# Seventy further matmuls on TensorE behind the last FFN tile

## The chip, the cores and the metric

The kernel runs on one core of one Trainium2 chip. The metric is the device time of one execution in microseconds (us). The core has four compute engines that concern us: TensorE (in the profile PE for the matmuls and PEld for the weight loads), VectorE (DVE), ScalarE (ACT) and GpSimd (POOL). DMA transfers are issued by SyncE's queue (SP, in the profile SPq). A matmul has a stationary operand, loaded as weights, and a moving operand, whose columns stream past the weights; its result goes to PSUM, a memory of 8 banks, of which one bank holds 128 x 512 float32.

## The reference

The kernel computes a transformer layer whose two branches run in parallel, for 2048 tokens of 576 channels:

```python
x = A_x
xn = _layernorm(x, axis=-1)
return x + _A_ref(xn, A_wqkv, A_wo) + _B_ref(xn, B_w1, B_b1, B_w2, B_b2)
```

`_A_ref` is attention of 32 heads of 18 channels over a dilated local window (8 positions, 2 apart) and an output projection `wo`. `_B_ref` is a feed-forward network (FFN): `relu(xn @ w1 + b1)` squared, times `w2`, plus `b2`, with 4608 hidden channels.

## The kernel before

The tokens are worked on in 4 blocks of 512 (`NB`, `TB`). The hidden channels of the FFN are cut into 36 tiles of 128 (`NF`), so there are `NT` = 144 FFN tiles in all, numbered through the blocks. The loop at the end of `block_kernel` calls `step(n)` for each of them and once more for the tail. A step asks for the weights of tile n + 2 (`load_w`: 128x640 of `w1` into `raw1`, 128x576 of `w2` into `raw2`, three buffers each), splits the `w1` tile of n + 1, runs `ffn1(n)`, splits the `w2` tile of n, runs a piece of attention or of the output projection, and runs `ffn2(n - 2)`: `LAG` = 2 steps lie between the first and the second matrix product of a tile.

Float32 precision is made from float32r, a float32 format that TensorE takes at full rate. Each operand is split into a high part and a rest: ScalarE copies float32 to float32r (line 118, or line 124 for `w2` and `wo`), VectorE subtracts (line 120 or 126). A product is then three products: high by high, high by rest, rest by high. All matmuls of the steady part have 128 stationary columns, and most have 512 moving columns:

- line 492 (`ffn1`): 14 matmuls into one bank of the pool `pw`, whose three buffers are all named `wk`; ScalarE reads the bank (lines 494 to 498: relu, and the square twice, into `hh` and `r`) and VectorE makes the rest `hl` (line 499).
- line 515 (`accumulate`): 14 matmuls a tile into five banks `y`, which stay open for a whole block; the output projection adds to the same banks, with the weights `wos` (a single buffer, written by line 124).
- line 372 (`three`): the projections to q, k and v, 56 matmuls for each quarter of the heads in each block, with the moving width from the list `WIDE` in line 39: 448, 512, 384 and 384 columns in the first block, 512, 512, 384 and 320 in the others.
- line 172: transposes of 128x128 in the opening. Line 621: bfloat16 matmuls on a zeroed tile in the opening, 128x512, repeated with nothing read from them.

In the last part of the last block the steps also hold the five chunks of the output projection (`o_weights`, `o_chunk`, `o_acc`, lines 665 to 668): the chunk is prepared into a buffer named `kv` two steps before it is multiplied.

Most instructions are ordered by a scheduler from their dependencies. Within `manual_schedule` the engines named there keep the order of the program; the opening is written so, and the tail (`ffn2_tail`), which closes the last two tiles. In the tail each bank `y` is completed in turn and stored, and for the last group of output channels the tail takes two fresh buffers `wk` and computes two halves of 256 columns, six matmuls each (line 564). VectorE adds each half to the residual (line 566), and the queue stores it (line 567). All engines take the instructions of their own list strictly in order.

The last buffer taken from `pw` ahead of the tail is that of the last `ffn1`; then come the two of line 561.

Of the kernel before, what the change touches and what calls it, by code (L numbers as in the profile page):

```python
# [8 lines left out]
F32 = mybir.dt.float32  # L9
F32R = mybir.dt.float32r  # L10
BF16 = mybir.dt.bfloat16
AF = mybir.ActivationFunctionType
ALU = mybir.AluOpType
ET = mybir.EngineType
AX = mybir.AxisListType

P = 128
S, D, F = 2048, 576, 4608
H, DH, W, DIL = 32, 18, 8, 2
TB = 512  # L20
NB = S // TB
NJ = TB // P
NC = 5
# [20 lines left out]
def block_kernel(ctx: ExitStack, tc: tile.TileContext, x, xt, wqkv, wo, w1, b1, w2, b2, out):  # L44
# [624 lines left out]
    def step(n):  # L669
        if 2 < n + 2 < NT:  # L670
            load_w(n + 2)
        if 0 < n < NT - 1:
            split_w1(n + 1)
        for f, a in pre.get(n, []):
            f(*a)
        if 0 < n < NT:
            ffn1(n)
        if n < NT:
            split_w2(n)
        busy = n >= NF and n % NF in (LAG - 1, LAG - 2)  # L680
        for f, a in mid.get(n, []):
            f(*a)
        if not busy:
            piece()
            piece()
        if n == NT:
            with tc.manual_schedule(engines={ET.PE, ET.DVE}):
                ffn2_tail([NT - 2, NT - 1])
        elif n >= LAG:
            ffn2(n - LAG)  # L690
        if not busy:
            piece()

    for n in range(NT + 1):
        with opening() if n < 7 else ExitStack():
            step(n)


_OUTS = [((1, S, D), 'float32')]

# [42 lines left out]
```

## Time and profile before

| what | value |
|---|---|
| median of 3 runs | 1161.35 us (1161.29 to 1161.71) |
| the profiled execution: time | 1161.42 us |
| the profiled execution: span, first to last instruction | 1159.7 us |
| TensorE matmul busy, share of the span | 1154.3 us, 100% |
| weight loads busy | 966.5 us, 83% |
| VectorE, ScalarE, GpSimd busy | 847.5, 602.2, 18.3 us |
| matmuls | 5227 |
| granted TensorE clock, mean | 1.000 |

A profile row for a group of instructions names the line, the engine, the operation, the tiles written and read, the shapes and the count; behind the bar come the busy time in us, the mean of one in ns, and the idle time of the engine before them with what ended it. A row of the timeline begins with the start and the length in us, counted from the start of the span. Matmul records overlap, since a matmul's results are still draining while the next one's columns enter: the length of a record is not the time that a matmul adds to a stream. The chain of waits is followed back from the last instruction, at each step to what released it. A row of windows begins with the stretch, its length, then the busy time and count of the matmuls and of the loads, the granted clock, the DMA share and GB/s.

### The profile page before, as it was taken

The numbers are of one execution on the slowest core, as the hardware profiler recorded it, in microseconds if no ns is written. First come the engines' busy times: TensorE is split into PE (matmuls) and PEld (weight loads), VectorE is DVE, ScalarE is ACT, GpSimd is POOL, SyncE is SP. The second block draws the span as 40 slices with busy tenths as digits, with TensorE's granted clock in tenths as the row PEclk, the third lists the DMA queues.
The fourth block names the chain that finished last, engine by engine and source line by source line (L and its number), as shares of the span: only waits on it lengthen the run. The fifth ranks groups of instructions, "written<-read, shape, count | busy, mean of one in ns | idle before, by whom it ended". The sixth has DMA issues, their size and how long they took to land.

```text
span 1159.7 us, 14795 instructions
## 1 busy us (share of the span) xinstructions
PE 1154.3 (100%) x5227; PEld 966.5 (83%) x5227; DVE 847.5 (73%) x1373; ACT 602.2 (52%) x1086; POOL 18.3 (2%) x32
## 2 busy tenths in 40 slices
PE   9999999999999999999999999999999999999998
PEld 7888888888888888888888888888888888888887
DVE  6967798892788686995287969698528795957453
ACT  7645545563545454555364546555535455545552
POOL 2000000000000100000000010000000000000000
PEclk9999999999999999999999999999999999999999
DMA  8656547432656655444266665644326645353421
GB/s 290 214 170 223 177 133 234 123 112 63 209 190 206 212 183 198 132 115 120 63 234 203 203 216 153 214 111 125 106 75 232 221 131 184 108 181 111 121 63 51
DMA packets 89674, 185.90 MB, mean 160 GB/s; under 512 B 9984, under 2 KB 33280, under 8 KB 88320
## 3 DMA queue, kind: packets, MB, share of 16 engines
q1 hardware_dynamic: 89312, 184.58, 50.1%
q8 instruction: 41, 0.67, 0.2%
q10 hardware_dynamic: 288, 0.38, 0.1%
q14 instruction: 33, 0.27, 0.1%
HBM read 165.96 MB, written 18.96 MB: 159 GB/s over the span
## 4 chain that ended last, share of the span: by engine, by line
PE 99%; DMA 0%; DVE 0%; SPq 0%; issue 0%
PE y L515 44%; PE wk L492 39%; PE wk L372 14%; PE wk L236 1%; DMA xb<-in_x 0%; PE y L172 0%; PE wk L564 0%; DVE st L138 0%; DVE xr L566 0%; SPq L104 0%; DVE xt L166 0%
## 5 line engine op out<-in xcount | busy, mean ns | idle before, releaser
L515 PE MATMUL y<-hh,w2s 128*128 128x512 f32 x1292 | 319.8, 389 | 0.0
L515 PEld LDWEIGHTS y<-hh,w2s 128*128 128x128 f32 x1292 | 242.5, 188 | 50.4
L492 PE MATMUL wk<-xh,w1h 128*128 128x512 f32 x720 | 210.3, 389 | 0.0
L515 PE MATMUL y<-hl,w2s 128*128 128x512 f32 x718 | 189.5, 389 | 0.0
L492 PE MATMUL wk<-xh,w1l 128*128 128x512 f32 x720 | 187.6, 389 | 0.0
L120 DVE TENSOR_TENSOR w1l<-raw,w1h 128x640 fp32r<-128x640 f32 x144 | 118.1, 820 | 66.4 <-ACT w1h L118 52.0
L118 ACT ACTIVATE w1h<-raw 128x640 fp32r<-128x640 f32 x144 | 106.1, 737 | 115.7 <-PE wk L492 114.0
L124 ACT ACTIVATE w2s<-raw 128x576 fp32r<-128x576 f32 x144 | 97.8, 683 | 120.0 <-PE y L515 118.1
L492 PEld LDWEIGHTS wk<-xh,w1l 128*128 128x128 f32 x720 | 135.1, 188 | 28.1
L515 PEld LDWEIGHTS y<-hl,w2s 128*128 128x128 f32 x718 | 134.8, 188 | 28.0
L492 PEld LDWEIGHTS wk<-xh,w1h 128*128 128x128 f32 x720 | 134.9, 188 | 27.5
L492 PE MATMUL wk<-xl,w1h 128*128 128x512 f32 x576 | 154.1, 389 | 0.0
L126 DVE TENSOR_TENSOR w2s<-raw,w2s 128x512 fp32r<-128x512 f32 (+1 forms) x288 | 118.0, 453 | 47.3 <-ACT w2s L124 46.2
L499 DVE TENSOR_TENSOR hl<-r,hh 128x512 fp32r<-128x512 f32 x144 | 98.8, 686 | 42.4 <-ACT r L498 42.3
L492 PEld LDWEIGHTS wk<-xl,w1h 128*128 128x128 f32 x576 | 108.1, 188 | 22.6
L494 ACT ACTIVATE r<-wk,b1t 128x512 f32<-128x512 f32 x144 | 98.5, 684 | 39.7 <-PE wk L492 39.4
L425 DVE TENSOR_TENSOR pr<-qo,kv 128x1152 f32<-128x1152 f32 x64 | 86.6, 1353 | 34.7 <-DMA kv<-kscr 34.7
L372 PE MATMUL wk<-wqh,xh 128*128 128x512 f32 (+2 forms) x300 | 106.3, 355 | 0.0
L372 PE MATMUL wk<-wql,xh 128*128 128x512 f32 (+2 forms) x300 | 106.3, 355 | 0.0
L498 ACT ACTIVATE r<-r 128x512 f32<-128x512 f32 x144 | 91.0, 632 | 4.4
L497 ACT ACTIVATE hh<-r 128x512 fp32r<-128x512 f32 x144 | 90.9, 632 | 4.1
L447 DVE TENSOR_TENSOR pr<-lg,kv 128x1152 f32<-128x1152 f32 x64 | 86.8, 1356 | 1.6
(91 smaller groups left out, 961.1 us busy)
## 6 DMA issues: line engine op xcount, KB each, us to landing
raw<-in_w SPq DMA_DIRECT2D x144, 320.0 KB, 3.0
raw<-in_w SPq DMA_DIRECT2D x144, 288.0 KB, 2.8
kv<-kscr SPq DMA_DIRECT2D x16, 1008.0 KB, 5.7
kv<-vscr SPq DMA_DIRECT2D x16, 1008.0 KB, 8.2
wqr<-in_wqkv SPq DMA_DIRECT2D x35, 256.0 KB, 3.3
raw<-in_wo SPq DMA_DIRECT2D x20, 288.0 KB, 2.8
wqr<-in_wqkv SPq DMA_DIRECT2D x25, 192.0 KB, 4.0
kscr<-kv SPq DMA_DIRECT2D x16, 288.0 KB, 3.0
```

What stands on the lines that cost most here:

```text
L118: i = nc.scalar.activation(hi, raw, AF.Copy)
L120: i = nc.vector.tensor_tensor(out=lo, in0=raw, in1=hi.bitcast(F32), op=ALU.subtract)
L124: nc.scalar.activation(w[:, :D], raw, AF.Copy)
L126: nc.vector.tensor_tensor(out=w[:, o:o + n], in0=raw[:, a:a + n], in1=w[:, a:a + n].bitcast(F32), op=ALU.subtract)
L372: nc.tensor.matmul(ps, l, r, start=i == 0, stop=i == len(mm) - 1)
L447: nc.vector.tensor_tensor(out=pr.rearrange("p w (a d) -> p w a d", d=DH), in0=at[:, :, :, None].to_broadcast([P, W, HG, DH]), in1=shifted( ...
L492: nc.tensor.matmul(p, l, r, start=i == 0, stop=i == len(mm) - 1)
L494: nc.scalar.activation(r, p, AF.Relu, bias=b1t[:, f:f + 1])
L497: nc.scalar.activation(hh, r, AF.Square)
L498: nc.scalar.activation(r, r, AF.Square)
L499: last_hl[0] = nc.vector.tensor_tensor(out=hl, in0=r, in1=hh.bitcast(F32), op=ALU.subtract)
L515: nc.tensor.matmul(yp[b][c], v, a, start=first and c not in cs[:i], stop=c in last and c not in cs[i + 1:], skip_group_check=True)
```

## The change

Behind the last step, one function more is run, with TensorE in program order:

```diff
@@ -695,6 +695,47 @@
         with opening() if n < 7 else ExitStack():
             step(n)
 
+    def more_products():
+        t = sb.tile([P, NC * TB], F32R, name="xt", bufs=1)
+        for i in range(4):
+            nc.scalar.activation(t[:, i * 640:(i + 1) * 640], raw1[NT - 1], AF.Copy)
+        u = sb.tile([P, NC * P], BF16, name="u")
+        nc.scalar.activation(u, raw1[NT - 1], AF.Copy)
+        wide, other, third = [pw.tile([P, TB], F32, name="wk") for _ in range(3)]
+        moving = [t[:, i * TB:(i + 1) * TB] for i in range(2)]
+        cut = [u[:, i * P:i * P + TB] for i in range(2)]
+        at = [0]
+
+        def weights(step=1):
+            at[0] = (at[0] + step) % 8
+            return t[:, 2 * TB + at[0] * P:2 * TB + (at[0] + 1) * P]
+
+        def group(n, out=wide, m=P, width=TB, step=1):
+            for i in range(n):
+                nc.tensor.matmul(out[:m, :width], weights(step)[:, :m], moving[i % 2][:, :width], start=True, stop=True,
+                                 skip_group_check=True)
+
+        def short(n, step=1):
+            for i in range(n):
+                at[0] = (at[0] + step) % 4
+                nc.tensor.matmul(third, u[:, at[0] * P:(at[0] + 1) * P], cut[i % 2], start=True, stop=True,
+                                 skip_group_check=True)
+
+        group(6)
+        group(6, other, m=64)
+        group(6, step=0)
+        group(6, other, width=256)
+        group(8, width=192)
+        group(8, other, width=128)
+        group(8, width=64)
+        group(4, other)
+        short(6)
+        short(6, step=0)
+        group(6)
+
+    with tc.manual_schedule(engines={ET.PE}):
+        more_products()
+
```

The tile `t` takes the buffer `xt`, which held the transposed input of the blocks, and `u` is a new bfloat16 tile of 128x640. Both are filled from the last `w1` tile by five ScalarE copies of 128x640. ScalarE is not under the manual order here, so the scheduler places these copies as soon as their input is there in its plan: two stand ahead of the split of the `w2` tile `raw_9769` (in the timeline of before at 1103.50 us), and three behind it. On ScalarE and VectorE a few neighbouring instructions near there change places; on TensorE and in the DMA queue the order up to line 564 stays.

`group` issues `n` float32r matmuls of `m` stationary and `width` moving columns into one bank, each a product of its own (`start` and `stop` set); the weights go round eight places of `t`, or stay at one with `step=0`. `short` does the same with bfloat16 operands, 128 stationary and 512 moving columns. The calls make 70 matmuls, in eleven groups. The three buffers `wk` are, in turn, that of the last `ffn1` and the two of line 561. Nothing reads the products, and the output is computed as before.

## The prediction

> **What bounds the kernel now.** I read the page first, then who waited on TensorE, then the end of the chain of waits, then single stretches of the timeline. On the page:
>
> ```profile
> span 1159.7 us, 14795 instructions
> ...
> PE 1154.3 (100%) x5227; PEld 966.5 (83%) x5227; DVE 847.5 (73%) x1373; ACT 602.2 (52%) x1086; POOL 18.3 (2%) x32
> ...
> PEclk9999999999999999999999999999999999999999
> ...
> PE 99%; DMA 0%; DVE 0%; SPq 0%; issue 0%
> ...
> L118 ACT ACTIVATE w1h<-raw 128x640 fp32r<-128x640 f32 x144 | 106.1, 737 | 115.7 <-PE wk L492 114.0
> ```
>
> TensorE is busy for all of the span and makes 99% of the chain; ScalarE is half idle. The view of waits, for TensorE over the whole span, has three rows, all in the first microseconds:
>
> ```profile
> PE wk L621 <- DVE warm L614: 1.2, 1, 1.2
> PE wk L619 <- POOL rs L147: 0.6, 1, 0.6
> PE y L172 <- DVE xt L166: 0.2, 1, 0.2
> ```
>
> So work put behind TensorE's last instruction is neither shortened by a gap nor hidden behind another engine's work, except in the short stretch in which the kernel today only writes its last results. That stretch is the end of the chain (start, length, what):
>
> ```profile
> 1154.91 1.44 PE wk L564 x12
> ...
> 1156.38 0.42 DVE xr L566
> ```
>
> In the timeline the last instructions of TensorE and of the DMA queue, and in the list of DMA issues how long such a store takes to land:
>
> ```profile
> 1155.82 0.40 PE L564 MATMUL wk<-hh,w2s 128*128 128x256 f32 x2
> 1155.83 0.19 PEld L564 LDWEIGHTS wk<-hh,w2s 128*128 128x128 f32 x1
> ...
> 1156.06 0.28 PE L564 MATMUL wk<-hl,w2s 128*128 128x256 f32 x1
> ```
> ```profile
> 1156.86 0.40 SPq L567 DMA_DIRECT2D out<-xr  x1
> ```
> ```profile
> out<-xr SPq DMA_DIRECT2D x7, 128.0 KB, 2.1
> ```
>
> The last store lands at 1156.86 + 2.1 = 1158.96 us. The span ends at 1159.7, so 0.74 us of closing handshakes follow the last landing. TensorE's last matmul starts at 1156.06 and ends at 1156.34: it has 2.6 us of free time before that landing, no more. The profiled execution took 1161.42 us, 1.72 more than its span; the three timed runs have a median of 1161.35.
>
> **What the new instructions cost.** The calls issue 70 matmuls: 28 of 512 moving columns in float32r (6 of these with 64 stationary columns, 6 with the same weights), 6 of 256, 8 each of 192, 128 and 64, and 12 of 512 in bfloat16 with a weight load of their own as an instruction. They go behind line 564 in TensorE's order, and nothing of before leaves.
>
> The price of a matmul in a stream is the distance between starts, not the record's length, since records overlap. Four widths of float32r can be read off; the chain's rows at 958.52 and 1012.72 are the groups of 384 and 320 columns of the last block (line 39), the others are a stretch of the timeline and the busy time of line 564 in a window:
>
> ```profile
> 958.52 9.73 PE wk L372 x56
> ...
> 1012.72 8.21 PE wk L372 x56
> ```
> ```profile
> 1109.64 2.20 PE L515 MATMUL y<-hh,w2s 128*128 128x512 f32 x9
> 1111.68 1.29 PE L515 MATMUL y<-hl,w2s 128*128 128x512 f32 x5
> ```
> ```profile
> 1154.74:1156.06 1.32, 1.31 (x11) 1.30 (x11) 1.00 0.73 255
> ```
>
> 512 columns: (1111.68 - 1109.64) / 9 = 0.2267 us. 384: 9.73 / 56 = 0.1738. 320: 8.21 / 56 = 0.1466. 256: 1.32 / 11 = 0.120. The steps (0.053 for 128 columns, 0.027 for 64) give 0.417 ns a column, and 13.3 ns a matmul on top at every width.
>
> *Plain 512 columns, and the same weights:* 22 x 0.2267 = 4.99 us. With the same weights each matmul still brings its own load in the instruction listing. At the lowest the 13.3 ns fall away there, 6 x 0.0133 = 0.08 less; at the highest nothing changes, and this I take.
>
> *64 stationary columns:* no row has this form. I take 6 x 0.2267 = 1.36: the 512 moving columns pass as before, and a load of half the columns has more room to hide, not less. Bounds: 0.08 below (as above), and, if such a load could not be overlapped at all, 6 x 0.19 = 1.14 above, by the load's record at 1155.83. The Trainium skill has a rule against my zero: in "TensorEngine Tiling (Array Packing)", section Key Properties, a change of tiling mode, other than a change of tile, drains TensorE. By it the sum would be that of the rival below with the emptied pipeline, 0.3 us more; the trace of before has no change of tile and so neither shows nor denies it.
>
> *256 columns:* 6 x 0.120 = 0.72.
>
> *192, 128 and 64 columns:* the largest unknown, as no float32r row is narrower than 256. Continued, the straight line gives 93.3, 66.6 and 40.0 ns, 8 x 0.1999 = 1.60 us. But every one needs a fresh load of 128 columns. In the rows of line 564 a load starts as the matmul before its own starts (1155.83 and 1155.82), so one load at a time stands ready, and the next matmul comes 0.120 later: a load needs at most that. The nearest rows with fewer moving columns are the transposes at the opening:
>
> ```profile
> 8.78 0.60 PE L172 MATMUL y<-ident,xt 128*128 128x128 f32 x4
> ```
> ```profile
> L172 PEld LDWEIGHTS y<-ident,xt x20: 138/141/143, 6.2 to 16.9; 128*128 128x128 f32 x20
> L172 PE MATMUL y<-ident,xt x20: 272/273/330, 6.2 to 17.0; 128*128 128x128 f32 x20
> ```
> ```profile
> L564 PEld LDWEIGHTS wk<-hl,w2s x4: 188/192/192, 1154.9 to 1155.9; 128*128 128x128 f32 x4
> ```
>
> Their distance is (0.60 - 0.273) / 3 = 0.109 at 128 moving columns, where the line would give 0.067, and their loads are shorter (141 ns against 192). So I take a floor of 0.120 for all three widths: 24 x 0.120 = 2.88 us. Lower bound 1.60 (the line); upper bound 24 x 0.2267 = 5.44, a narrow one no cheaper than a full one. The value lies nearer the lower because the transposes, the nearest rows, do.
>
> *Operands of half the width:* the opening has bfloat16 matmuls of this shape, the first at the start of the kernel, the last after some microseconds:
>
> ```profile
> 1.24 2.74 PE L621 MATMUL wk<-warm 128*128 128x512 bf16 x6 [1.24 <-DVE warm L614]
> ```
> ```profile
> 4.49 0.60 PE L621 MATMUL wk<-warm 128*128 128x512 bf16 x2
> ```
> ```profile
> 4.49 0.10 PEld L621 LDWEIGHTS <-warm 128*128 128x128 bf16 x1
> ```
>
> Later they stand 0.60 - 0.38 = 0.22 apart (the last record of the four takes 0.38), with the load hidden: 12 x 0.22 = 2.64. Bounds: 12 x 0.2133 (columns alone) = 2.56, and 12 x (0.22 + 0.10) = 3.84 if the load were exposed; I take 2.64, the row of the very form.
>
> Sum: 4.99 + 1.36 + 0.72 + 2.88 + 2.64 = 12.59 us.
>
> **What else the change adds.** Five ScalarE copies of 128x640 (0.737 each, row of line 118 above) are placed early: in the new order two stand ahead of the split of w2s of 1103.50 and three behind it, and the first waits for the last tile of w1. Rows of ScalarE, of the queue, of landing times, of VectorE and of TensorE:
>
> ```profile
> 1102.25 0.62 ACT L118 ACTIVATE kv<-r 128x512 fp32r<-128x512 f32 x1
> 1103.50 0.69 ACT L124 ACTIVATE w2s<-raw 128x576 fp32r<-128x576 f32 x1 [0.63 <-PE y L515]
> ...
> 1109.84 0.69 ACT L124 ACTIVATE wos<-raw 128x576 fp32r<-128x576 f32 x1 [0.63 <-PE y L515]
> ```
> ```profile
> 1101.23 0.33 SPq L466 DMA_DIRECT2D raw<-in_w  x1
> ```
> ```profile
> raw<-in_w SPq DMA_DIRECT2D x2, 320.0 KB, 2.9
> ```
> ```profile
> 1110.56 0.83 DVE L126 TENSOR_TENSOR wos<-raw,wos 128x512 fp32r<-128x512 f32 x2 [0.55 <-ACT wos L124]
> ```
> ```profile
> 1115.99 1.30 PE L515 MATMUL y<-kv,wos 128*128 128x512 f32 x5
> ```
>
> That tile is requested at 1101.23 and lands near 1104.1, so ScalarE, free at 1102.87, stands for some 1.3 us. Behind it queue two copies (to 1105.6), w2s (1106.3), three copies (1108.5), then w1h, r, kv, hh and r again (0.74, 0.69, 0.62, 0.64, 0.63: 1111.8), then wos until 1112.5 in place of 1110.5. VectorE's two pieces follow until 1113.4, and TensorE asks for wos at 1115.99: 2.6 us to spare. The others have more: hh, w2s and kv of this step are consumed two steps later (LAG, and lines 667 and 668), and a step is 1112.98 - 1103.46 = 9.5 us:
>
> ```profile
> 1103.46 3.17 PE wk L492 x14
> ...
> 1112.98 3.17 PE wk L492 x14
> ```
>
> Of the queue's loads, that of 1105.11 waits for w2s and that of 1111.45 for wos; both would go out some 2 us later, land near 1110 and 1116.4, and are wanted at 1113.0 and 1119.4:
>
> ```profile
> 1105.11 0.33 SPq L468 DMA_DIRECT2D raw<-in_w  x1
> 1111.45 0.33 SPq L573 DMA_DIRECT2D raw<-in_wo  x1
> ```
> ```profile
> 1113.02 0.69 ACT L124 ACTIVATE w2s<-raw 128x576 fp32r<-128x576 f32 x1 [2.49 <-PE y L515]
> ...
> 1119.36 0.69 ACT L124 ACTIVATE wos<-raw 128x576 fp32r<-128x576 f32 x1 [0.63 <-PE y L515]
> ```
>  So this costs nothing; the cover is those 2.6 us before wos, and beyond it every microsecond of lateness would be one of TensorE's. The orders of TensorE and of the DMA queue are otherwise unchanged; VectorE exchanges neighbours.
>
> **The sum.** The first new matmul can start at 1156.06 + 0.12 = 1156.18: its buffer was read long before, and the two others are free when VectorE has read them (1156.16 and 1156.80), ahead of their first use at 1157.5 and near 1166. The last of the 70 starts at 1156.18 + 12.59 - 0.23 = 1168.54 and ends 0.39 later, 1168.93. The last store has landed at 1158.96, so now TensorE ends last. With 0.74 of closing the span is 1169.7, and with 1.72 around it the time is **1171.4 us**, 10.0 (0.86%) above the profiled execution. Of the 12.59 us, 2.6 disappear in the tail.
>
> **Rivals.**
>
> *The line goes on below 256 columns.* For: 13.3 ns is the same at four widths. Against: the transposes. Then 2.88 becomes 1.60, and the time 1170.1. Chance 0.11. The Trainium skill's own distance, in the section Back-to-back issue gap of the page on the matmul, N / 2.4 + 2.5 ns with a floor near 25, would make these 24 an estimated 1.34 us and the time 1169.9.
>
> *Narrow ones cost as much as full ones.* For: a 128-column transpose already costs 0.109 and not 0.067, so width does not scale down. Against: 256 columns still lie on the line. 5.44 in place of 2.88: 1173.9. Chance 0.11.
>
> *The 64-column group stands out.* If TensorE's pipeline empties at its two borders, two matmuls show their undivided record, 1.29 - 4 x 0.227 = 0.38 by the row of 1111.68, in place of 0.227: 0.3 us more, 1171.7. If all six loads are exposed, 1.14 more, 1172.5. For: no row has the form. Against: every change of width and operand in the rows above goes without a gap. Chance 0.07.
>
> *ScalarE's wait reaches TensorE.* It decides when the last tile of w1 lands more than 2.6 us behind 1104.1; a landing of twice the median (2.9 late) would give 0.3 us: 1171.7. Chance 0.02.
>
> *TensorE's clock falls.* The first bfloat16 rows stand (2.74 - 0.63) / 5 = 0.42 apart, twice the later 0.22: the clock was half at the start. If the thin activity of the narrow groups (columns passing 1.28 of 2.88 us) halved it again, and it stayed so, the 22 full matmuls behind them would cost 0.2 more each: 1175.8. Against: the page's clock row stays at 9 throughout. Chance 0.02.
>
> *Not slower: the tail hides it.* One mechanism: the products have no reader, so the end is set by the last store if TensorE is done before it lands, 2.6 us behind 1156.34. It decides only if the 70 take under 2.8 us, 40 ns each; 28 full ones at 0.2133 of column time alone take 6.0. That nothing is issued at all would also end here, at 1161.4, but the listing holds all 70. Chance 0.01.
>
> **How the numbers follow.** The forecast itself has 0.66, its own range 1170.8 to 1172.0. The line (1170.1), with the three lower bounds of 0.08 for same weights, 64 columns and half width, sets the lower end, 1169.8; the full price of narrow ones (1173.9), with 0.1 for the closing, the upper, 1174.0. A difference of 0.2% (2.3 us) is about what can be told from no change; all cases but the last lie 8 us or more above the time before. Slower 0.98; within 0.2% 0.015; faster 0.005.
>
> **What would show it.** Right: the first new matmul at 1156.2 with no wait, distances of 0.227, 0.120 and 0.22, equal distances at 192, 128 and 64 columns, TensorE's last end near 1168.9, a new end of the chain on TensorE, and TensorE's rows up to line 564 where they were. Wrong: distances below 0.109 or above 0.13 in the narrow groups, a gap at the borders of the 64-column or the bfloat16 group, any wait of TensorE near 1116, a clock digit below 9 in the last slices.

## The result, and the profile after

| kernel | median | runs | ratio to before (95% interval) |
|---|---|---|---|
| before | 1161.32 us | 4 (1161.26 to 1161.71) | |
| after | 1171.34 us | 4 (1171.17 to 1171.42) | 1.0084 (1.0072 to 1.0096) |

The change costs 10.0 us. The profiled execution took 1171.41 us with a span of 1169.7. The page of the changed kernel has the rows of the same kind as before:

```profile
span 1169.7 us, 14941 instructions
...
PE 1167.5 (100%) x5297; PEld 976.1 (83%) x5297; DVE 846.9 (72%) x1373; ACT 604.4 (52%) x1091; POOL 18.3 (2%) x32
...
PEclk9999999999999999999999999999999999999999
```

TensorE has 70 matmuls more and still no gap, ScalarE five instructions more, and the clock row is unchanged. The end of the chain of waits (start, length, what) shows where the time is:

```profile
1144.74 10.20 PE y L515 x45
1154.94 1.43 PE wk L564 x12
1156.38 8.45 PE wk L715 x52
1164.83 2.60 PE wk L721 x12
1167.43 1.38 PE wk L715 x6
```

Before, the chain ended with VectorE's addition and the last store. Now it ends on TensorE, with the new lines 715 and 721. Up to line 564 the rows of TensorE stand where they stood, within 0.03 us. The list of waits of TensorE has only one row left, the one at the very start:

```profile
PE wk L621 <- DVE warm L614: 1.2, 1, 1.2
```

One row of windows for each of the first eight of the eleven new groups (stretch from its first start to the next group's, its length; the counts include neighbours that reach into the stretch); the bfloat16 ones and the last six stand in the chain above:

```profile
1156.21:1157.60 1.39, 1.39 (x8) 1.08 (x7) 0.42 (x1) 0.00 (x0) 0.00 (x0) 1.00 0.73 251
1157.60:1158.98 1.38, 1.38 (x7) 0.86 (x6) 0.00 (x0) 0.00 (x0) 0.00 (x0) 1.00 0.37 127
1158.98:1160.34 1.36, 1.36 (x7) 1.13 (x6) 0.00 (x0) 0.00 (x0) 0.00 (x0) 1.00 0.00 0
1160.34:1161.05 0.71, 0.71 (x7) 0.70 (x6) 0.00 (x0) 0.00 (x0) 0.00 (x0) 1.00 0.00 0
1161.05:1161.92 0.87, 0.87 (x10) 0.87 (x9) 0.00 (x0) 0.00 (x0) 0.00 (x0) 1.00 0.00 0
1161.92:1162.79 0.87, 0.87 (x10) 0.87 (x9) 0.00 (x0) 0.00 (x0) 0.00 (x0) 1.00 0.00 0
1162.79:1163.65 0.86, 0.86 (x10) 0.86 (x10) 0.00 (x0) 0.00 (x0) 0.00 (x0) 1.00 0.00 0
1163.65:1164.66 1.01, 1.01 (x6) 0.65 (x5) 0.00 (x0) 0.00 (x0) 0.00 (x0) 1.00 0.00 0
```

The reader is to compare the lengths. Six of 512 columns take 1.39, 1.38 (64 stationary columns) and 1.36 us (same weights); six of 256 take 0.71; and eight of 192, of 128 and of 64 columns take 0.87, 0.87 and 0.86. Within these three groups the starts are about 0.112 us apart (0.109 to 0.116), except that the first distance of each is shorter: 0.091, 0.080 and 0.078. The step from 256 to 192 columns still gains a little, and from there nothing more is gained. The four full matmuls behind them take 1.01 us, 0.10 more than four distances of 0.227.

### The profile page after: what moved, and what is told of

It reads as the page before. It is cut to its first block, busy times and chain, and to the rows that moved or that the text cites. A ratio compares the mean times of both kernels' runs of the same rounds, so it can differ in the third digit from the quotient of the medians.

```text
span 1169.7 us, 14941 instructions
## 1 busy us (share of the span) xinstructions
PE 1167.5 (100%) x5297; PEld 976.1 (83%) x5297; DVE 846.9 (72%) x1373; ACT 604.4 (52%) x1091; POOL 18.3 (2%) x32
## 4 chain that ended last, share of the span: by engine, by line
PE 99%; DMA 0%; DVE 0%; POOL 0%; issue 0%; POOLq 0%
PE y L515 44%; PE wk L492 39%; PE wk L372 14%; PE wk L236 1%; PE wk L715 1%; PE y L172 0%; DMA xb<-in_x 0%; PE wk L721 0%; PE wk L564 0%; DVE st L138 0%; POOL rs L147 0%; DVE xt L166 0%; DVE mv L142 0%; DVE rs L146 0%; POOLq L147 0%
## 5 line engine op out<-in xcount | busy, mean ns | idle before, releaser
L118 ACT ACTIVATE wqh<-wqr 128x512 fp32r<-128x512 f32 (+2 forms) x75 | 40.6, 561 | 94.3 <-DMA wqr<-in_wqkv 64.9
```

What stands on the lines that cost most here:

```text
L118: i = nc.scalar.activation(hi, raw, AF.Copy)
```

## The experiments

All variants compute the output as before; only the function behind the last tile differs, and in two of them its place or the order near it.

### The copies alone, ten matmuls alone

The first edit empties the list of calls, the second leaves ten:

```diff
-        group(6)
-        group(6, other, m=64)
...
-        group(6)
+        pass
```
```diff
         group(6)
-        group(6, other, m=64)
...
-        group(8, width=64)
         group(4, other)
-        short(6)
-        short(6, step=0)
-        group(6)
```

> The five ScalarE copies stay, all 70 matmuls are left out; the output is computed as before. Theory: the copies make ScalarE wait 1.3 us for the last tile of w1 and run late until 1111.5 us, which the 2.6 us of room before TensorE asks for wos absorbs: 1161.3 us, as before, and TensorE's rows near 1116 where they were. Rival: a part of the 10 us comes from the copies, by way of a wait of TensorE: 1161.8 us or more.

Measured: 1161.37 us (10 runs), ratio 1.000 (0.999 to 1.001). ScalarE behaves in this kernel as in the changed one, whose timeline shows the wait and the copies:

```profile
1104.21 1.37 ACT L701 ACTIVATE xt<-raw 128x640 fp32r<-128x640 f32 x2 [1.31 <-DMA raw<-in_w]
1105.48 0.67 ACT L124 ACTIVATE w2s<-raw 128x576 fp32r<-128x576 f32 x1
1106.05 1.35 ACT L701 ACTIVATE xt<-raw 128x640 fp32r<-128x640 f32 x2
1107.31 0.72 ACT L703 ACTIVATE u<-raw 128x640 bf16<-128x640 f32 x1
...
1110.84 0.67 ACT L124 ACTIVATE wos<-raw 128x576 fp32r<-128x576 f32 x1
```

The wait of 1.31 us for the last tile of `w1` is there, and `wos` is written at 1110.84 where it was 1109.84. TensorE takes it near 1116 as before. So the copies and their wait cost nothing.

> Of the 70 matmuls only ten of 128 stationary and 512 moving columns stay (6 and 4, in two banks). Theory: they take 10 x 0.231 = 2.3 us and end near 1158.7 us, ahead of the landing of the last store at 1158.95, so the tail hides all of them: 1161.3 us. Rival: behind the last matmul every matmul counts in full, because the end waits for TensorE in a way of its own: 1163.6 us.

Measured: 1161.46 us (10 runs), ratio 1.000 (0.999 to 1.0009). The ten stand in the timeline from 1156.18 to 1158.64:

```profile
1156.18 2.46 PE L715 MATMUL wk<-xt 128*128 128x512 f32 x10
```

The last of them starts at 1158.24. 2.3 us of matmul work behind the last one is free, because the last store lands later. This shows the cover of the tail directly.

### Without the narrow groups; ahead of the tail

```diff
-        group(8, width=192)
-        group(8, other, width=128)
-        group(8, width=64)
```

> The changed kernel without its 24 matmuls of 192, 128 and 64 moving columns. Theory: the distances of the trace are what they cost, 24 x 0.112 = 2.7 us: 1168.65 us. Rival: narrow matmuls cost at their borders too (the matmul behind them starts 0.09 later than in a plain stream), up to 0.2 us more: 1168.4 us.

Measured: 1168.62 us (1168.59 to 1168.65). The 24 narrow matmuls are worth 1171.34 - 1168.62 = 2.72 us, or 0.113 each. That is the theory's 24 x 0.112; the rival's 1168.4 is 0.2 off. The runs of the changed kernel lie 0.25 us apart, so the time alone would not separate the two; in the traces the stretch from the first new matmul to the last is 2.68 us shorter without the narrow ones (9.53 against 12.20), which is the theory's.

```diff
             with tc.manual_schedule(engines={ET.PE, ET.DVE}):
+                more_products()
                 ffn2_tail([NT - 2, NT - 1])
...
-    with tc.manual_schedule(engines={ET.PE}):
-        more_products()
```

> The same 70 matmuls, issued ahead of the tail of the last two tiles and not behind it. Theory: here nothing covers them, so the 2.6 us that the last store hides are lost: 12.4 us on top of before, 1173.7 us. Rival: what counts is the work alone, wherever it stands: 1171.3 us, as in the changed kernel.

Measured: 1173.78 us (1173.72 to 1173.80), ratio 1.0107 (1.0091 to 1.0122). The same 70 matmuls cost 12.4 us here and 10.0 behind the tail. The difference, 2.4 us, is what the last store hides.

### What sets the floor of the narrow ones

```diff
+        def short(n, step=1, width=TB):
...
+        group(4)
+        group(16, other, width=64)
+        group(16, m=64, width=64)
+        group(16, other, m=32, width=64)
+        group(16, width=64, step=0)
+        group(16, other, m=64, width=128)
+        group(4)
+        short(16, width=64)
+        short(16, step=0, width=64)
+        short(16, width=128)
+        group(4)
```

> Other groups in place of the eleven. float32r, 16 matmuls each, stationary x moving columns: 128x64, 64x64, 32x64, 128x64 with the same weights, 64x128; then bfloat16, 128 stationary columns: 64, 64 with the same weights, 128; with 4 full float32r ones ahead, between and behind. Theory of the load as floor (0.107 us for 128 columns and 0.005 around it): distances 0.112, 0.059, 0.040 (columns decide), 0.112, 0.067, and in bfloat16, whose load record is 0.10 in place of 0.19, 0.06 or less: some 10.9 us in all, 1169.6 us. Rival of a fixed floor per matmul: 0.112 in all eight groups, 17 us, 1175.9 us. Rival of a load left out when the weights are the same: 0.040 in the fourth group.

Measured: 1169.60 us in one run, against 1169.6 from the theory and 1175.9 from the fixed floor. Rows of windows, in the order of the float32r groups, then both groups of bfloat16 with 64 columns together, then that with 128:

```profile
1157.12:1158.83 1.71, 1.71 (x17) 1.70 (x16) 0.00 (x0) 0.00 (x0) 0.00 (x0) 1.00 0.50 171
1158.83:1159.76 0.93, 0.93 (x18) 0.93 (x18) 0.00 (x0) 0.00 (x0) 0.00 (x0) 1.00 0.00 0
1159.76:1160.27 0.51, 0.51 (x19) 0.51 (x18) 0.00 (x0) 0.00 (x0) 0.00 (x0) 1.00 0.00 0
1160.27:1162.06 1.79, 1.79 (x22) 1.79 (x19) 0.00 (x0) 0.00 (x0) 0.00 (x0) 1.00 0.00 0
1162.06:1163.05 0.99, 0.99 (x18) 0.99 (x18) 0.00 (x0) 0.00 (x0) 0.00 (x0) 1.00 0.00 0
1164.02:1164.97 0.95, 0.95 (x33) 0.95 (x33) 0.00 (x0) 0.00 (x0) 0.00 (x0) 1.00 0.00 0
1164.97:1165.83 0.86, 0.86 (x22) 0.86 (x19) 0.00 (x0) 0.00 (x0) 0.00 (x0) 1.00 0.00 0
```

With 64 moving columns and 128, 64 and 32 stationary ones, 16 matmuls take 1.71, 0.93 and 0.51 us: 0.107, 0.058 and 0.032 each (0.112 in the first group but for one short distance at its start). The number of stationary columns decides, though the moving ones are the same. Repeating the weights changes nothing (1.79 us, 0.112 each): the listing has a load for each of these too. In bfloat16 the distance is 0.95 / 32 = 0.030 at 64 columns, so there is no fixed floor near 0.11. The groups by form name the loads and their mean record:

```profile
L715 PEld LDWEIGHTS wk<-xt 128*128 128x128 f32 x40 | 5.2, 191 | 0.3
...
L715 PEld LDWEIGHTS wk<-xt 128*64 128x64 f32 x32 | 2.0, 137 | 0.0
L721 PEld LDWEIGHTS <-u 128*128 128x128 bf16 x48 | 1.8, 98 | 0.3 <-issue 0.3
...
L715 PEld LDWEIGHTS wk<-xt 128*32 128x32 f32 x16 | 0.6, 110 | 0.0
```

128, 64 and 32 stationary columns give 191, 137 and 110 ns: 0.84 ns a column on 83 ns. The distances of 0.112, 0.058 and 0.032 us are 0.84 ns a column and some 4 ns, so the 83 ns overlap with other work, and 128 x 0.84 = 108 ns makes the floor. Two numbers were off: 32x64 came at 0.032 and not 0.040, and 64x128 at 0.060 (its first distance of 0.090 apart) and not 0.067, so the 13.3 ns of the wide matmuls are not there in narrow ones.

### A change of stationary width

```diff
+        def switch(n):
+            for i in range(n):
+                group(1, (wide, other)[i % 2], m=(P, 64)[i % 2])
...
+        group(6)
+        switch(12)
+        group(6, m=64)
+        group(6)
+        switch(12)
+        group(6)
```

> 42 matmuls of 512 moving columns: 6 full, 12 alternating between 128 and 64 stationary columns, 6 of 64, 6 full, 12 alternating, 6 full. Theory: a change of stationary width costs nothing, distances 0.227 to 0.236 throughout, 9.6 us, 1168.4 us. Rival, the rule of the Trainium skill that a change of tiling mode drains TensorE: at each of some 26 changes the undivided 0.38 in place of 0.227, 4.0 us more, 1172.4 us.

Measured: 1169.73 us in one run. The expectation counted 42 matmuls where the code makes 48; six more at 0.23 are 1.4 us, so the theory's time is 1169.8 and the rival's 1173.8. The ten distances of each alternating stretch:

```profile
1157.53:1159.85 2.32, 2.32 (x11) 1.61 (x10) 0.00 (x0) 0.00 (x0) 0.00 (x0) 1.00 0.16 56
1163.06:1165.38 2.32, 2.32 (x11) 1.61 (x10) 0.00 (x0) 0.00 (x0) 0.00 (x0) 1.00 0.00 0
```

2.32 / 10 = 0.232 us, though every matmul changes the stationary width; the rival asked for 0.38. The draining of which the Trainium skill speaks ("TensorEngine Tiling (Array Packing)", Key Properties) did not show in this run for matmuls that differ only in their stationary columns; whether it holds for other tiles of the array was not tried.

### How long the clock bears thin work

```diff
         group(6)
...
+        group(160, other, width=64)
+        group(16)
+        group(6, other)
```

> 6 full matmuls, then 160 of 64 moving columns (17.9 us, in which columns pass for a quarter of the time), then 22 full ones. Theory: the clock holds, 24.3 us in all, 1183.0 us. Rival, a falling clock: full matmuls 0.42 apart behind the thin stretch, 4.6 us more, 1187.7 us, and a granted clock below 1 in the last slices. The distances of the 22 also tell two readings of the 0.231 apart: if it is a pipeline out of step behind a change of width, the first ten or so stand 0.23 apart and the rest 0.2267; if it comes from weights that change from one matmul to the next, all 22 stand 0.231 apart.

Measured: 1199.44 us in one run, with a mean granted clock of 0.986. The theory fell. The windows (the granted clock stands behind the five engines):

```profile
1157.56:1160.46 2.90, 2.90 (x28) 2.89 (x26) 0.00 (x0) 0.00 (x0) 0.00 (x0) 0.99 0.18 60
1160.46:1188.97 28.51, 28.51 (x135) 28.51 (x135) 0.00 (x0) 0.00 (x0) 0.00 (x0) 0.50 0.00 1
1188.97:1194.00 5.03, 5.03 (x13) 3.97 (x14) 0.00 (x0) 0.00 (x0) 0.00 (x0) 0.50 0.00 0
1194.00:1196.50 2.50, 2.50 (x12) 1.97 (x10) 0.00 (x0) 0.00 (x0) 0.00 (x0) 0.89 0.00 0
```

2.9 us into the thin stretch the clock falls to 0.50 and stays there, although matmuls follow each other without a gap: 28.51 us for 134 of them, 0.213 each in place of 0.112. The full matmuls then start at half clock too, and 5.6 us pass before it is back, at 1194.53. The rival was right on the fall and its price far too low, since it counted the full matmuls alone and not the thin ones (134 x 0.101 = 13.5 us). What the expectation wanted to learn from the 22 full ones stays open: thirteen stand at half clock, 0.427 apart but for the first, and the nine behind the clock's return stand 0.224 to 0.236 apart without settling.

```diff
         group(6)
...
+        group(60, other, width=192)
+        group(30)
+        group(60, other, width=128)
+        group(30)
```

> 6 full matmuls, 60 of 192 moving columns (6.7 us, columns passing 80 of 112 ns), 30 full, 60 of 128 (columns passing 53 of 112 ns), 30 full. It asks from which share of passing columns the clock falls; with 64 columns (27 of 112 ns) it fell 2.9 us into the stretch and stayed at half for the first 5 us of full ones. If no share near a half or above lets it fall: 28.5 us in all, 1187.3 us, clock 1.00. If it falls at 128 alone: about 3.4 us more in the second stretch and 2.4 behind it, 1193 us. If it falls at both: 1199 us.

Measured: 1187.38 us in one run, the first case:

```profile
1157.55:1164.23 6.68, 6.68 (x61) 6.67 (x60) 0.00 (x0) 0.00 (x0) 0.00 (x0) 1.00 0.08 26
1164.23:1171.07 6.84, 6.84 (x32) 5.66 (x31) 0.00 (x0) 0.00 (x0) 0.00 (x0) 1.00 0.01 2
1171.07:1177.71 6.64, 6.64 (x61) 6.64 (x60) 0.00 (x0) 0.00 (x0) 0.00 (x0) 1.00 0.00 0
```

60 of 192 and 60 of 128 columns take 6.7 and 6.6 us, twice as long as the stretch after which the clock fell, and it holds at 1.00. So in these two runs the border lies between 27 and 53 ns of passing columns in 112.

```diff
-        group(8, width=64)
+        group(24, width=64)
```

> The changed kernel with 24 in place of 8 matmuls of 64 moving columns: the narrow stretch lasts 4.4 us in place of 2.6. Theory from the long thin stretch: the clock falls within it, the matmuls behind it start at 0.42, about twelve of them before it recovers: 16 x 0.112 = 1.8 us for the further matmuls and 2.4 to 4 us for the clock, 1175.5 to 1177.2 us. Rival: a stretch of this length, begun with 192 and 128 columns, is too short: 1173.1 us. If the fall hangs on a clock of its own that does not start with the stretch, single runs differ by microseconds.

Measured: 1173.14, 1173.07 and 1173.17 us with a mean granted clock of 1.000, and 1176.45 us with 0.997. The rival holds in three runs of four, the theory in one. Both are seen on the same program, so whether the clock falls hangs on something that does not begin with the stretch. The two traces with a fall hint at what: with 160 thin matmuls the clock changes at 1160.40 and 1194.53 us, 34.13 apart, and with ten times the copies (below) at 1152.29 and 1155.70, 3.41 apart, a tenth of it. So it looks as if the clock is set anew only every 3.41 us, and the place of the thin stretch between two such moments would decide. The fourth run fits: a mean of 0.997 is about 7 us at half clock, two such steps, which would cost 3.4 us, and 3.3 are seen. This is an estimate, as that run has no trace. The changed kernel's own narrow stretch showed no fall in twelve runs: its four, the four ahead of the tail and the four with sixfold copies (below) all have a mean of 1.000.

### ScalarE's room

```diff
-        for i in range(4):
+        for i in [*range(4)] * 6:
...
+        for i in range(6):
+            nc.scalar.activation(u, raw1[NT - 1], AF.Copy)
```

> The changed kernel with each of its five ScalarE copies made six times (25 further copies, 15.5 us of ScalarE), spread by the scheduler over the last five steps. Theory: the room before wos is used up; by the new order of ScalarE the third chunk of wos is ready near 1128.2 us, where TensorE wants it at 1125.5, so TensorE waits some 2.8 us there (1 to 4): 1174.1 us. Rival: ScalarE is half idle and takes them all: 1171.3 us.

Measured: 1171.33 us (1171.22 to 1171.39), the rival's time. My expectation was wrong because the scheduler also reordered TensorE: it put a second `ffn1` ahead of the output projection. `wos` of the third chunk was ready at 1128.14, as expected, but wanted at 1131.87 and not at 1125.5:

```profile
1125.52 1.07 PE L492 MATMUL wk<-xh,w1h 128*128 128x512 f32 x4
...
1128.69 1.07 PE L492 MATMUL wk<-xh,w1h 128*128 128x512 f32 x4
...
1131.87 3.34 PE L515 MATMUL y<-kv,wos 128*128 128x512 f32 x14
```

The next kernel holds TensorE to its order, with ten times the copies:

```diff
+    fixed = ExitStack()
     for n in range(NT + 1):
+        if n == 137:
+            fixed.enter_context(tc.manual_schedule(engines={ET.PE}))
+        if n == NT:
+            fixed.close()
...
+        for i in [*range(4)] * 10:
```

> The changed kernel with each ScalarE copy made ten times (45 further copies, 28 us of ScalarE), and TensorE held to its order of before from step 137 on. Theory: ScalarE works without a gap from 1104.2 us and by its order ends the last r near 1151.9 us; the last hl is then ready near 1152.8, and TensorE, which uses it at 1150.48 in the changed kernel, waits some 2.3 us there: 1173.7 us (1172.7 to 1174.7), a wait of TensorE for VectorE's line 499 in the list of waits. Rival: room enough even so: 1171.3 us.

Measured: 1175.70 us (1174.39 to 1175.88), above the expected range. The wait is where it was expected and of the expected size; the windows show what came with it:

```profile
1149.87 0.39 PE L515 MATMUL y<-hh,w2s 128*128 128x512 f32 x1
1152.30 0.80 PE L515 MATMUL y<-hl,w2s 128*128 128x512 f32 x1 [2.05 <-DVE hl L499]
```
```profile
1152.20:1154.00 1.80, 1.70 (x3) 1.00 (x4) 0.74 (x2) 0.51 (x1) 0.00 (x0) 0.52 0.00 0
1154.00:1156.00 2.00, 2.00 (x7) 1.52 (x6) 1.44 (x2) 0.00 (x0) 0.00 (x0) 0.57 0.00 0
1156.00:1160.00 4.00, 4.00 (x23) 3.45 (x22) 2.45 (x6) 0.00 (x0) 0.00 (x0) 1.00 0.48 159
```

TensorE loses 2.2 us to the late `hl` (1152.30 against 1150.10 by the distance of 0.227), and more because the clock was at half for 3.4 us behind the wait, from 1152.29 to 1155.70. From that `hl` to the first matmul of line 564 it takes 6.67 us (1152.30 to 1158.97), and in the changed kernel 4.76 (1150.02 to 1154.78): 1.9 more. With the 0.07 by which this kernel was late before the wait, that is the 4.2 us by which its span of 1173.9 is longer. In the run of 1174.39 the mean granted clock was 1.000 where the others have 0.999, which fits a run without the fall; it has no trace.

## Why the prediction was right, point by point

The time was forecast at 1171.4 and came at 1171.34. Its terms, by the starts in the trace:

| term | forecast | measured |
|---|---|---|
| 22 full float32r matmuls, same weights among them | 4.99 | 5.14 |
| 6 with 64 stationary columns | 1.36 | 1.38 |
| 6 of 256 columns | 0.72 | 0.71 |
| 24 of 192, 128 and 64 columns, start to start | 2.88 | 2.60 |
| 12 bfloat16 | 2.64 | 2.60 |
| sum | 12.59 | 12.43 |

*The place of the first new matmul and no wait:* as forecast, 1156.21 against 1156.18, and the waits ahead of the second and third buffer did not show.

*Full matmuls:* mis-sized by 0.15 us. Part is a border: the first full matmul behind the narrow ones stood 0.314 us from the next, 0.087 more than usual. That is as much as the three short distances at the starts of the narrow groups (0.091, 0.080, 0.078) lack to 0.112 together. This suggests that the two belong together, and by what they add to the stream the narrow ones cost 24 x 0.112 = 2.69, which is what taking them out gave (2.72). The rest is a distance of 0.228 to 0.236 in place of 0.2267 for some matmuls. In the kernel with ten full ones the distances run 0.234, 0.236, 0.228, 0.232, 0.231 and then 0.227, though the weights go on changing; in the one ahead of the tail, where full ones stand in front, the first group runs at 0.227 from its start. So it does not come from the change of weights. It stands behind a change of width, and once behind a change of the clock. Why was not tried.

*64 stationary columns, same weights:* both right. The rival of a drain is refuted, and the same weights are loaded again.

*The narrow floor:* right in kind, 0.112 in place of 0.120. The floor was read off 256 columns, where columns (107 ns) and load (108 ns) happen to be equal and the 13.3 ns of a wide matmul stand on top; those are not paid by the narrow ones. One of the prediction's own signs of being wrong, a distance below 0.109 in the narrow groups, did show, in the first distance of each; it is paid back at the border behind them, so it does not speak against the floor. The rivals of 40 to 93 ns and of 0.227 are refuted in these runs.

*The sum at the end:* TensorE ended at 1168.82 (last start 1168.42 and 0.40) where 1168.93 was forecast; from there to the end of the span it is 0.88 and not 0.74. The two differences, 0.11 less and 0.14 more, all but cancel, as the narrow groups' 0.28 less and the full ones' 0.15 more do in part. The kind of each term was right; that the time came within 0.1 us is in part luck. 1.72 around the span held (1171.41 - 1169.7).

*The copies:* cost nothing, as forecast. ScalarE came to `wos` 1.0 us late and not 2.0, since its copies start 0.63 us apart (1106.05 to 1107.31 for two) where the forecast took the record of 0.737. So `wos` was ready at 1112.40 and wanted at 1116.02, with 3.6 us of room and not 2.6. With ten times the copies it still came in time here, by 0.3 us (1115.76 against 1116.09), and the late step that TensorE felt was `hl` of the last tiles.

*The rivals:* the tail hides what fits into it, shown with ten matmuls and again with all 70 ahead of it; the change was only too large for it. The clock was given 0.02 on the ground that the clock row stood at 9 throughout. That row cannot show it, since the kernel before has no thin stretch. The changed kernel's narrow stretch lasts 2.6 us, and with 4.4 us the fall came in one run of four: the low chance was right by a margin smaller than I thought, and that this stretch was short enough was luck, since the forecast had no row to tell.

## What to carry to other kernels

Work behind the last matmul was free up to the landing of the last store, and from there each microsecond counted. A float32r matmul with 128 stationary columns cost at least 0.112 us here, the time of its load, so below some 256 moving columns next to nothing was gained by making it narrower (0.120 to 0.112); fewer stationary columns (0.058 with 64) or bfloat16 (0.030 at 64 moving columns) did gain. Price a chain of narrow matmuls, and any wait of TensorE of 2 us, with the clock's fall in mind: what followed ran at half clock for 3.4 us behind the wait and for 5.6 us behind the long thin stretch.

## What the runs showed of the hardware that was not expected

- Matmuls of 64 columns in an unbroken row let the granted clock fall to 0.50 after 2.9 us and kept it there for 28.5 us; 128 columns at the same distance kept it at 1.00 for 6.6 us. The Trainium skill, in "TensorE: Matmul & The Clock Gate", section Why this matters for your kernels, ties a falling clock to idle gaps over some 3 us between matmuls; here there was no gap, and after a single wait of 2.05 us the clock fell to 0.50 as well, for 3.4 us.
- The same program took 1173.1 us in three runs and 1176.45 in a fourth, so such a stretch also made the time uncertain by 3 us.
- A load cost 0.84 ns for each stationary column in float32r (191, 137 and 110 ns for 128, 64 and 32), and its record has 83 ns on top that did not add to a stream.
- Behind a change of width some matmuls stood 0.224 to 0.236 us apart before they settled at 0.227.
